# Attention, gate and experts on one core: the product with w_out as seven products of quarters, with prepared weights kept in DRAM

## The chip, the core and the metric

The kernel runs on 1 core of one Trainium2 chip. The time is that of the core on the device, in microseconds (us); 831.33 is the median of three runs, which lie between 831.1 and 831.34. TensorE (PE in the profile, its weight loads PEld) multiplies, VectorE (DVE) and ScalarE (ACT) compute on SBUF and on PSUM, where TensorE's results land, GpSimd (POOL) computes on SBUF and issues its own DMAs, and SyncE (SP) issues the other DMAs. Each engine works through its own queue in order and waits on semaphores.

## The reference, cut to what matters

Three blocks follow each other, on 1536 tokens (2 x 768) with 512 features:

```
x   = local attention of q, k, v, mem_k, mem_v           # chunks of 32 tokens, 8 heads of 64
y   = (sigmoid(x @ w_gate) * (x @ w_val)) @ w_out        # 512 -> 1536 -> 512
out = sum over 4 experts e of  p[:, e] * (relu(y @ w1[e]) @ w2[e])   # 512 -> 1024 -> 512
```

p is domain_probs divided by its row sums. Everything is float32. w_gate, w_val and w_out arrive as 64-bit floats, whose bits the kernel turns into 32-bit floats itself.

## The kernel before, in words

Every matmul operand is split into a high part (a cast to fp32r, on ACT) and a low part (the rest, a subtraction on VectorE), and a product is three matmuls: high x high, high x low, low x high (`mm3`, lines 177 to 180). TensorE's queue therefore sees triples of lines 178, 179 and 180.

The order of all work is written out by hand (`manual_schedule`): the program's order is each engine's queue order. The stages are:

- Attention, with the first value projections (`pv`) filled in between.
- The gating stage. For each of 12 row blocks f of w_out's input and three chunks c of 512 tokens, `g_part` makes the gate product, a sigmoid (line 1093) and the multiplication with the value (line 1099). The result lies in `g_t[f]`, one tile of 1536 tokens for each f. Between chunks, `dec` advances the weights of later products: per block two VectorE operations and one of ACT that rebuild 32-bit floats from the 64-bit words (lines 133, 139, 143), then the high cast and the low subtraction (lines 168, 172). A gate block f < 8 takes 12 matmuls a chunk, f >= 8 takes 24, since the value product is made there too.
- The product with w_out (`pb`, lines 1227 to 1253). For each chunk c of 512 tokens and each f, `g_split` splits the gated values three blocks ahead (lines 116 and 117) and four column blocks m of 128 are accumulated in four PSUM banks; at a chunk's end ACT copies them to `yr`. In the last chunk one step of `y_prep(0)` (the operands of the first half of y) and one of `w1_all(0)` (those of the first expert's w1) go behind each f.
- The expert block (`second_block`). Its products are already made by seven products of quarters instead of eight, with sums and differences of quarters as operands; y's seven operands for each token half are stored in DRAM (`kept_y`, line 364) and loaded back when a half is needed again.

In the last chunk VectorE's queue thus mixes three kinds of work: `hl` (gated values), `yo` and `yr` (y's operands and their sums, lines 245 and 248) and `w_s` and `raw` (w1's, lines 269 and 275). SP's queue mixes the stores of y with the loads of the raw w1 and w2 parts (lines 230 and 239). The casts of w2's first parts are made by line 332.

## Time and profile before

| what | value |
|---|---|
| time, median of 3 runs | 831.33 us |
| time of the profiled execution | 831.14 us |
| its span, first to last instruction | 829.1 us |
| TensorE busy | 823.2 us, 99% |
| VectorE busy | 541.4 us, 65% |
| ACT busy | 441.0 us, 53% |
| POOL busy | 163.8 us, 20% |
| TensorE's granted clock | 0.999 of full speed |

How to read it: an engine's busy time is a mean over stages. Whether an engine's work costs time is seen where another engine waits for it, and the row of a wait names the engine that waits, what it waits for and for how long. In the timeline the start of one matmul to the start of the next is what it costs TensorE; the recorded length overlaps with the next.

### The profile page before, as it was taken

To read this page: it belongs to the slowest core of one execution; us is meant where nothing else is said; L and a number is where in the kernel's file an instruction comes from. 1 tells how busy PE (TensorE), PEld (TensorE's weight loads), DVE (VectorE), ACT (ScalarE), POOL (GpSimd) and SP (SyncE) were. 2 spreads that over 40 slices of the span, in tenths; PEclk is the share of its full clock that TensorE was granted. 3 is DMA by queue.
4 is the path that set the end of the run, shared out by engine and by line. 5 is a ranking of instruction groups with operands and counts; after the bars stand their busy time and mean duration, and the time that the engine had idled before them with its cause. 6 is when DMAs were issued, how large, how long until landed. Compare 5 with 4: busy or idle time off the path is not lost.

```text
span 829.1 us, 14479 instructions
## 1 busy us (share of the span) xinstructions
PE 823.2 (99%) x5566; PEld 764.9 (92%) x5566; DVE 541.4 (65%) x1041; ACT 441.0 (53%) x953; POOL 163.8 (20%) x194
## 2 busy tenths in 40 slices
PE   8999999999999999999999999999999999999998
PEld 6899998888888888889899999999999999999998
DVE  7753246432343227565488788788888889888847
ACT  5764355331232326464566666666566666666642
POOL 3220000000000000010122532432342243243231
PEclk9999999999999999999999999999999999999999
DMA  9975053211110003554385794894893994994783
GB/s 345 342 284 164 2 153 117 87 51 47 56 51 1 0 1 157 211 226 168 127 308 86 121 341 62 143 346 49 164 321 42 221 268 47 261 225 54 232 193 77
DMA packets 47845, 127.47 MB, mean 154 GB/s; under 512 B 5648, under 2 KB 27552, under 8 KB 47776
## 3 DMA queue, kind: packets, MB, share of 16 engines
q1 hardware_dynamic: 23888, 102.53, 33.9%
q0 software_dynamic: 23888, 24.02, 20.5%
q8 instruction: 43, 0.70, 0.3%
q14 instruction: 26, 0.21, 0.1%
HBM read 90.35 MB, written 36.18 MB: 153 GB/s over the span
## 4 chain that ended last, share of the span: by engine, by line
PE 97%; DMA 1%; ACT 1%; DVE 1%; issue 0%; POOL 0%; SPq 0%; ACTq 0%; DVEq 0%; POOLq 0%
PE b L178 5%; PE b L179 5%; PE b L180 5%; PE B L180 5%; PE B L179 5%; PE B L178 5%; PE pv L178 4%; PE pv L180 4%; PE pv L179 4%; PE pg L180 4%; PE pg L178 4%; PE pb L180 4%; PE pb L178 4%; PE pb L179 4%; PE pg L179 4%; PE e L178 3%
## 5 line engine op out<-in xcount | busy, mean ns | idle before, releaser
L662 POOL DMA_DIRECT2D out_dram<-st x159 | 137.4, 929 | 267.6 <-DVE st L685 238.4
L178 PE MATMUL b<-yo,w_s 128*128 128x384 f32 x256 | 86.7, 339 | 0.2
L179 PE MATMUL b<-yo,w_s 128*128 128x384 f32 x256 | 86.6, 338 | 0.0
L180 PE MATMUL b<-yo,w_s 128*128 128x384 f32 x256 | 86.4, 337 | 0.0
L269 DVE TENSOR_TENSOR w_s<-raw,w_s 128x512 fp32r<-128x512 f32 x105 | 69.4, 685 | 8.9 <-ACT w_s L263 8.9
L553 POOL DMA_DIRECT2D out_dram<-st x12 | 6.5, 543 | 337.2 <-ACT st L552 337.0
L263 ACT CAST w_s<-raw 128x512 fp32r<-128x512 f32 x105 | 61.1, 618 | 14.8 <-DVE raw L275 14.7
L1093 ACT ACTIVATE sg<-pg 128x512 f32<-128x512 f32 x36 | 21.5, 598 | 84.3 <-PE pg L180 84.3
L178 PE MATMUL pv<-xs,w_v 128*128 128x384 f32 (+1 forms) x176 | 64.2, 365 | 0.0
L622 DVE SCALAR_TENSOR_TENSOR v<-v 128x384 f32<-128x384 f32 x112 | 61.9, 553 | 2.1 <-ACT v L775 0.6
L180 PE MATMUL pv<-xs,w_v 128*128 128x384 f32 (+1 forms) x176 | 61.8, 351 | 0.0
L179 PE MATMUL pv<-xs,w_v 128*128 128x384 f32 (+1 forms) x176 | 61.5, 349 | 0.0
L117 DVE TENSOR_TENSOR hl<-g,hl 128x512 fp32r<-128x512 f32 x36 | 24.7, 690 | 48.5 <-ACT hl L116 48.5
L180 PE MATMUL pg<-xs,w_g 128*128 128x512 f32 x144 | 56.0, 389 | 0.0
L179 PE MATMUL pg<-xs,w_g 128*128 128x512 f32 x144 | 56.0, 389 | 0.0
L178 PE MATMUL pb<-hl,w_o 128*128 128x512 f32 x144 | 56.0, 389 | 0.0
L179 PE MATMUL pb<-hl,w_o 128*128 128x512 f32 x144 | 56.0, 389 | 0.0
L180 PE MATMUL pb<-hl,w_o 128*128 128x512 f32 x144 | 56.0, 389 | 0.0
L178 PE MATMUL pg<-xs,w_g 128*128 128x512 f32 x144 | 56.0, 389 | 0.0
L116 ACT CAST hl<-g 128x512 fp32r<-128x512 f32 x36 | 22.2, 623 | 54.8 <-PE pb L180 54.8
L178 PEld LDWEIGHTS b<-yo,w_s 128*128 128x128 f32 x256 | 48.2, 188 | 1.3 <-ACT s L466 0.9
L179 PEld LDWEIGHTS b<-yo,w_s 128*128 128x128 f32 x256 | 48.2, 188 | 0.3
(278 smaller groups left out, 2435.5 us busy)
## 6 DMA issues: line engine op xcount, KB each, us to landing
yo<-kept_y SPq DMA_DIRECT2D x49, 768.0 KB, 10.3
out_dram<-st POOLq DMA_DIRECT2D x159, 128.0 KB, 4.6
raw<-in_w_dram SPq DMA_DIRECT2D x32, 512.0 KB, 6.9
kept_y<-yo SPq DMA_DIRECT2D x14, 768.0 KB, 4.2
kv<-in_kvc_dram SPq DMA_DIRECT2D x20, 483.0 KB, 6.0
raw<-in_w_v_dram SPq DMA_DIRECT2D x12, 512.0 KB, 6.9
raw<-in_w_g_dram SPq DMA_DIRECT2D x12, 512.0 KB, 5.5
raw<-in_w_o_dram SPq DMA_DIRECT2D x12, 512.0 KB, 3.2
```

Source lines behind the costliest of these rows:

```text
L116: nc.scalar.copy(out=hi, in_=src)
L117: nc.vector.tensor_tensor(out=lo, in0=src, in1=f32(hi), op=ALU.subtract)
L178: nc.tensor.matmul(out=ps, lhsT=w_hi, rhs=r_hi, start=first, stop=False, skip_group_check=more)
L179: nc.tensor.matmul(out=ps, lhsT=w_hi, rhs=r_lo, start=False, stop=False, skip_group_check=more)
L180: nc.tensor.matmul(out=ps, lhsT=w_lo, rhs=r_hi, start=False, stop=last, skip_group_check=more)
L263: nc.scalar.copy(out=high(t), in_=parts(n)[a])
L269: nc.vector.tensor_tensor(out=low(t), in0=parts(n)[a], in1=f32(high(t)), op=ALU.subtract)
L553: nc.gpsimd.dma_start(out=out_of(n, tt, slice(0, DM)), in_=st)
L622: nc.vector.scalar_tensor_tensor(out=out, in0=x, scalar=0.0, in1=y, op0=ALU.max, op1=op)
L662: nc.gpsimd.dma_start(out=out_of(n, t, cols_of(dh)), in_=st, accum_op=ALU.add)
L1093: nc.scalar.activation(out=sg, in_=ps, func=AF.Sigmoid)
```

## The change

The product with w_out is made in two rounds of 768 tokens. Each round makes seven products of quarters (tokens in halves of 384, w_out's rows in halves of six blocks, its columns in halves of 256), in the order 1, 7, 6, 2, 5, 4, 3 (`M_USE`). A product takes three slots c; a slot pairs row blocks and has 12 matmuls of 384 columns. The list of pieces:

- w_out is decoded in pairs (p, p + 6) of row blocks; `o_prep` makes four sums and seven operands of a pair, in eleven steps, and stores each operand to DRAM (`kept_o`, 42 stores of 256 KB). `jobs` lists these 66 steps among the nine that are left for w_gate and w_val, and a number per gating chunk is issued: one in two of three chunks for f < 4, three for f < 8, five for f < 11. `o_load` brings a product's operands back, three loads of 512 KB, issued two products ahead.
- The gated values lie in `g_t[j, f // 2]`, a tile for each token half j, so one chunk's multiplication may be cut in two. The sums of their quarters are made in place: `sum1` and `sum3` on VectorE, `sum2` and `sum4` on POOL. `o_split` splits the operand of a slot one product ahead.
- The last gating block makes its chunks 1 and 2 together, so that the tiles of x come free one by one.
- The steps of `y_prep(0)` and `w1_all(0)` go into the second round, at positions 3k + c. The sums in `y_prep(0)` are on POOL now.
- Tiles get other homes: the temporaries of attention and decoding lie in three tiles (`late`) that later hold three operands of y; weight tiles come from eight and four buffers (`w`, `ws`) in place of twelve.

The core of the diff:

```diff
+N_GV = 20
+M_USE = (1, 7, 6, 2, 5, 4, 3)
...
+    n_pr = KF // 2
+    pairs = [[("o", p), ("o", p + n_pr)] for p in range(n_pr)]
+    raw_order = order[:N_GV] + sum(pairs[:n_pr // 2], []) + order[N_GV:] + sum(pairs[n_pr // 2:], [])
+    raw_at = {key: i for i, key in enumerate(raw_order)}
...
-    def w_tile(pool, key):
-        W[key] = pool.tile([128, 2, 512], F32R, tag="w", name="w_" + "_".join(map(str, key)))
+    def w_tile(key):
+        tag, n = ("ws", 4) if NV <= order.index(key) < NV + 4 else ("w", 8)
+        W[key] = wp.tile([128, 2, 512], F32R, tag=tag, bufs=n, name="w_" + "_".join(map(str, key)))
...
+    late = ctx.enter_context(tc.tile_pool(name="late", bufs=3, side="right"))
...
+            tag, n = ("ws", 4) if 4 < made["w"] <= 8 else ("w", 8)
+            return wp.tile([128, 1024], F32R, tag=tag, bufs=n, name=f"w_s{made['w']}")
...
-        pool = tc.alloc_tile_pool(name="yo", bufs=1, side="right", reuse_waits="tile")
-        pools["yo"] = pool
         for m in (4, 5, 3):
-            op[m] = pool.tile([128, 2, 2, HT], F32R, name=f"yo{m}")
+            op[m] = late.tile([128, 2, 2, HT], F32R, tag="late", name=f"yo{m}")
...
-            q, t, do = y_sums(j, yr[j], nc.vector)
+            q, t, do = y_sums(j, yr[j], nc.gpsimd)
...
+        def g_ends(f, c, ps, val):
             sg = sgp.tile([128, CT], F32, tag="sg", bufs=3, name=f"sg{f}_{c}")
             nc.scalar.activation(out=sg, in_=ps, func=AF.Sigmoid)
-            val = g_t[f][:, ct(c)]
...
+        def g_part(f, cs):
+            todo = [("g", c, ps_tile(f"pg{f}_{c}")) for c in cs]
             if f >= NV:
...
+                todo += [("v", c, ps_tile(f"pv{f}_{c}")) for c in cs]
+            for k in range(KD):
+                for what, c, ps in todo:
+                    proj(ps, (what, f), ct(c), k)
...
+        kept_o = {m: kept.tile([128, n_pr, 2 * DH], F32, name=f"kept_o{m}") for m in M_USE}
+        DM2 = DM // 2
+        def o_prep(p):
+            t, w, o = {}, {}, []
+            def decoded(i):
+                def do():
+                    up, down = raw_parts(pairs[p][i])
+                    t2 = low_bits(down)
+                    t[i] = high_bits(i, up)
+                    joined(t[i], t2)
+                    raw_to(raw_at[pairs[p][i]] + 1 + RAWS)
+                return do
...
+            def hi(m, a):
+                def do():
+                    if len(w) % 2 == 0:
+                        o.append(wp.tile([128, 2, 2, DM2], F32R, tag="ws", bufs=4, name=f"o{p}_{m}"))
+                    w[m] = o[-1][:, len(w) % 2]
+                    nc.scalar.copy(out=w[m][:, 0], in_=part(a))
+                return do
+            def lo(m, a):
+                def do():
+                    nc.vector.tensor_tensor(out=w[m][:, 1], in0=part(a), in1=f32(w[m][:, 0]), op=ALU.subtract)
+                    nc.sync.dma_start(
+                        out=kept_o[m][:, p], in_=f32(w[m].rearrange("p l d -> p (l d)")))
+                return do
...
+            return [
+                decoded(0), decoded(1), both(hi(4, "a22"), hi(1, "a11")), both(lo(4, "a22"), s1),
+                both(hi(2, "a12"), lo(1, "a11"), s3, s2), both(lo(2, "a12"), s4), hi(7, "a21"),
+                both(hi(6, "a11"), lo(7, "a21")), both(hi(5, "a22"), lo(6, "a11")), both(hi(3, "a12"), lo(5, "a22")),
+                lo(3, "a12")]
...
+        jobs = [lambda n=n: split_f64(n) for n in range(begun[0], N_GV)] + [lambda: split_f64(N_GV, False)]
+        for p in range(n_pr // 2):
+            jobs += o_prep(p)
+        jobs += [lambda n=n: split_f64(n) for n in range(N_GV, n_64)] + [lambda: split_f64(n_64, False)]
+        for p in range(n_pr // 2, n_pr):
+            jobs += o_prep(p)
+        op_t, loaded = [], {}
+        def q_of(j, c):
+            k0, k1 = g_t[j, c], g_t[j, c + 3]
+            return dict(q00=k0[:, :, :HT], q01=k0[:, :, HT:], q10=k1[:, :, :HT], q11=k1[:, :, HT:], e=e_t[c])
+        def o_sum(j, c, eng, dst, a, b):
+            q = q_of(j, c)
+            eng.tensor_tensor(out=q[dst], in0=q[a], in1=q[b], op=ALU.subtract)
+        def sum1(j, c):
+            o_sum(j, c, nc.vector, "e", "q01", "q00")
+        def sum3(j, c):
+            o_sum(j, c, nc.vector, "q01", "q11", "q01")
+        def sum2(j, c):
+            o_sum(j, c, nc.gpsimd, "q00", "q11", "e")
+        def sum4(j, c):
+            o_sum(j, c, nc.gpsimd, "q00", "q10", "q00")
+        at_of = {1: "q00", 7: "q01", 6: "q00", 2: "q10", 5: "e", 4: "q00", 3: "q11"}
+        h_of = {}
+        def o_split(j, k, c):
+            m = M_USE[k]
+            op = op_t[(j * 7 + k) % 2 * 3 + c]
+            h_of[j, m, c] = op
+            a = q_of(j, c)[at_of[m]]
+            nc.scalar.copy(out=op[:, 0], in_=a)
+            nc.vector.tensor_tensor(out=op[:, 1], in0=a, in1=f32(op[:, 0]), op=ALU.subtract)
+        def o_load(i):
+            if i < 2 * 7:
+                m = M_USE[i % 7]
+                loaded[i] = [slot("w") for _ in range(3)]
+                for c in range(3):
+                    nc.sync.dma_start(
+                        out=f32(loaded[i][c]),
+                        in_=kept_o[m][:, 2 * c:2 * c + 2].rearrange("p a b -> p (a b)"))
+        for f in range(KF):
+            for cs in ((0,), (1,), (2,)) if f < KF - 1 else ((0,), (1, 2)):
+                ends = list(g_part(f, cs))
+                if f == KF - 1 and len(cs) > 1:
+                    ops = [xp.tile([128, 2, 2, 2, HT], F32R, tag="x", name=f"op{i}") for i in range(3)]
+                    op_t.extend(ops[i // 2][:, i % 2] for i in range(6))
+                    for c in range(3):
+                        o_split(0, 0, c)
+                for c, ps, val in ends:
+                    g_ends(f, c, ps, val)
+                n = 0
+                if f < 4:
+                    n = cs[0] != 1
+                elif f < NV:
+                    n = 3
+                elif f < KF - 1:
+                    n = 5
+                emit(jobs, n)
+                if f == NV:
+                    sum1(0, cs[0])
+                if f == NV + 1:
+                    if cs[0] == 0:
+                        sum3(0, 0)
+                if f == KF - 2 and cs[0] == 0:
+                    sum3(0, 1)
                 if f == KF - 1:
...
-            for c in range(NCT):
-                pss = [ps_tile(f"pb{c}_{m}") for m in range(KD)]
-                if c == NCT - 1:
-                    y_steps, w_steps = y_prep(0), w1_all(0)
-                for f in range(KF):
-                    i = c * KF + f
-                    g_split(i + 3)
-                    dec(begun[0])
-                    w, hl = W["o", f], hls.pop(i)
-                    for m in range(KD):
-                        mc = slice(m * 128, (m + 1) * 128)
-                        mm3(pss[m], w[:, 0, mc], w[:, 1, mc], hl[:, 0], hl[:, 1], f == 0, f == KF - 1)
-                    if c == NCT - 1:
-                        emit(y_steps, 1)
-                        emit(w_steps, 1 if f >= 2 else 0)
...
+                    if cs[0] == 0:
+                        emit(jobs, len(jobs))
+                        o_load(0)
+                        o_load(1)
+                    else:
+                        sum3(0, 2)
...
+        pos = {}
+        for j in range(NR):
+            if j == 1:
+                yr.append(xp.tile([128, KD, 2 * HT], F32, tag="x", name="yr1"))
+                yops.extend(y_ops())
+                raw1_load(0)
+                for i, do in enumerate(y_prep(0)):
+                    pos.setdefault(2 * i, []).append(do)
+                for i, steps in {
+                        8: "h4 h1", 9: "l4 s1", 10: "h2 l1 s3 s2", 11: "l2 s4", 15: "h7", 16: "h6 l7", 17: "l6 h5",
+                        18: "l5 h3", 19: "l3 x"}.items():
+                    pos.setdefault(i, []).append(lambda steps=steps: w1_do(0, steps))
+            ps = {}
+            for k, m in enumerate(M_USE):
+                i = j * 7 + k
+                o_load(i + 2)
+                name = {1: "b", 7: "e", 6: "b", 2: "a", 5: "b", 4: "e", 3: "b"}[m]
+                first = m in (1, 7, 2)
+                if first:
+                    ps[name] = [ps_tile(f"o{name}{j}_{u}") for u in range(2)]
+                if j == 0 and k == 6:
...
+                for c in range(3):
+                    if i + 1 < 2 * 7:
+                        o_split(*divmod(i + 1, 7), c)
+                    if k == 0:
+                        sum2(j, c)
+                    elif k == 1:
+                        sum4(j, c)
+                    elif j == 0 and k == 4:
+                        sum1(1, c)
+                    elif j == 0 and k == 5:
+                        sum3(1, c)
+                    if j == 1:
+                        for do in pos.get(3 * k + c, []):
+                            do()
+                    w = loaded[i][c].rearrange("p (a l d) -> p a l d", a=2, l=2)
+                    h = h_of[j, m, c]
+                    for a in range(2):
+                        for u in range(2):
+                            mc = slice(u * 128, (u + 1) * 128)
+                            n = 2 * c + a
+                            mm3(ps[name][u][:, :HT], w[:, a, 0, mc], w[:, a, 1, mc], h[:, 0, a], h[:, 1, a],
+                                first and n == 0, n == n_pr - 1, not first)
+                slots["w"].extend(loaded.pop(i))
+                for u in range(2):
+                    p = ps[name][u][:, :HT]
+                    t0, t1 = slice(0, HT), slice(HT, 2 * HT)
+                    y11, y21, y22, y12 = yr[j][:, u, t0], yr[j][:, 2 + u, t0], yr[j][:, 2 + u, t1], yr[j][:, u, t1]
+                    to = {1: y11, 7: y22, 6: y21, 2: y11, 5: y22, 4: y21, 3: y12}[m]
+                    if m in (1, 7, 6, 3):
+                        nc.scalar.copy(out=to, in_=p)
+                    else:
+                        nc.vector.tensor_tensor(out=to, in0=p, in1=to, op=ALU.add)
...
```

The scheduled orders show where this puts instructions. The first place is VectorE's queue beside the last quarter of the old product (row blocks 8 to 11 of the last chunk; `hl` is the split gated value, `yo` an operand of y, `w_s` an operand of w1, `raw1` its sums):

```order
L275 TENSOR_TENSOR raw1_0_2834<-raw1_1_2836,raw1_0_2834 128x512
L117 TENSOR_TENSOR hl32_3152<-g8_2213,hl32_3152 128x512
L245 TENSOR_TENSOR yo1_2841<-yr0_2839,yo1_2841 128x768
L269 TENSOR_TENSOR w_s3_3147<-raw1_0_2834,w_s3_3147 128x512
L275 TENSOR_TENSOR raw1_0_2834<-raw1_0_2834 128x512
L117 TENSOR_TENSOR hl33_3172<-g9_2311,hl33_3172 128x512
L245 TENSOR_TENSOR yo6_2842<-yr0_2839,yo6_2842 128x768
```

and now beside product 10, the fourth of the second round (`opb` is the split operand of product 11, one slot in a tile; the last row begins the results of product 10):

```order
L1325 TENSOR_TENSOR opb0_3030<-e0_1490,opb0_3030 128x768
L289 TENSOR_TENSOR w_s1_2633<-raw1_1_3088,w_s1_2633 128x512
L295 TENSOR_TENSOR raw1_1_3088<-raw1_1_3088 128x512
L1325 TENSOR_TENSOR opb1_3031<-e1_1491,opb1_3031 128x768
L265 TENSOR_TENSOR yo1_3081<-yr0_2715,yo1_3081 128x768
L289 TENSOR_TENSOR w_s2_2634<-raw1_0_3086,w_s2_2634 128x512
L295 TENSOR_TENSOR raw1_1_3088<-raw1_0_3086,raw1_1_3088 128x512
L295 TENSOR_TENSOR raw1_0_3086<-raw1_1_3088,raw1_0_3086 128x512
L1325 TENSOR_TENSOR opb2_3032<-e2_1492,opb2_3032 128x768
L289 TENSOR_TENSOR w_s6_2641<-raw1_0_3086,w_s6_2641 128x512
L295 TENSOR_TENSOR raw1_0_3086<-raw1_0_3086 128x512
L1429 TENSOR_TENSOR yr1_3080<-oa1_0_3263,yr1_3080 128x384
```

The splits have grown from 512 to 768 columns, y's sums (line 248 before) have left VectorE, and results of the product (line 1429) have come to it from ACT.

The second place is POOL's queue between its last low part of w_gate in the attention part and its first DMA of the expert block, before:

```order
L158 TENSOR_TENSOR w_g_2_1044<-t1_10_1004,w_g_2_1044 128x512
L158 TENSOR_TENSOR w_g_3_1141<-t1_11_1101,w_g_3_1141 128x512
L553 DMA out_0_dram<-st0_3295 128x512 x2
L553 DMA out_0_dram<-st1_3296 128x512 x2
L553 DMA out_0_dram<-st0_3295 128x512 x2
```

and now the part of the second round (`g1` is the second token half, `e` its first sum, `yr0` the first half of y):

```order
L1301 TENSOR_TENSOR g1_0_137<-g1_3_140,e0_1490 128x2x384
L1301 TENSOR_TENSOR g1_1_138<-g1_4_1656,e1_1491 128x2x384
L1301 TENSOR_TENSOR g1_2_139<-g1_5_1657,e2_1492 128x2x384
L268 TENSOR_TENSOR yr0_2715<-yr0_2715 128x2x384 x2
L1301 TENSOR_TENSOR g1_0_137<-g1_3_140,g1_0_137 128x2x384
L1301 TENSOR_TENSOR g1_1_138<-g1_4_1656,g1_1_138 128x2x384
L268 TENSOR_TENSOR yr0_2715<-yr0_2715 128x2x384
L1301 TENSOR_TENSOR g1_2_139<-g1_5_1657,g1_2_139 128x2x384
L268 TENSOR_TENSOR yr0_2715<-yr0_2715 128x2x384
```

POOL had nothing between the attention part and the expert block; it now has ten sums of 768 columns in this round, and six in the first.

The third place is SP's queue, from the stores of y to the loads of the raw w2 parts. Before, nothing stands between the last stores and the loads:

```order
L364 DMA kept_y0_78<-yo1_2841 128x1536
L364 DMA kept_y0_78<-yo6_2842 128x1536
L364 DMA kept_y0_78<-yo4_2846 128x1536
L230 DMA raw1_0_2834<-in_w_1_dram 128x1024
L230 DMA raw1_1_2836<-in_w_1_dram 128x1024
L239 DMA raw2_0_3291<-in_w_2_dram 128x1024
```

Now the operands of products 12 and 13 (`w_s` from `kept_o`) stand between the stores:

```order
L382 DMA kept_y0_83<-yo5_3084 128x1536
L1332 DMA w_s3_2635<-kept_o4_1652 128x1024
L1332 DMA w_s4_2639<-kept_o4_1652 128x1024
L1332 DMA w_s5_2640<-kept_o4_1652 128x1024
L382 DMA kept_y0_83<-yo1_3081 128x1536
L1332 DMA w_s7_2716<-kept_o3_1653 128x1024
L1332 DMA w_s8_2717<-kept_o3_1653 128x1024
L1332 DMA w_s9_2718<-kept_o3_1653 128x1024
L382 DMA kept_y0_83<-yo6_3082 128x1536
L382 DMA kept_y0_83<-yo4_3083 128x1536
L250 DMA raw1_0_3086<-in_w_1_dram 128x1024
L250 DMA raw1_1_3088<-in_w_1_dram 128x1024
```

Each product's loads are now queued behind a store that waits for a low part of y.

## Rows read from the trace of the kernel before

**Rows 1.** The page, engines' shares (busy us, share, instructions) and the chain by engine

```profile
PE 823.2 (99%) x5566; PEld 764.9 (92%) x5566; DVE 541.4 (65%) x1041; ACT 441.0 (53%) x953; POOL 163.8 (20%) x194
...
PE 97%; DMA 1%; ACT 1%; DVE 1%; issue 0%; POOL 0%; SPq 0%; ACTq 0%; DVEq 0%; POOLq 0%
```

**Rows 2.** Waits of TensorE: total us, times, longest

```profile
PE warm L964 <- DVE zero L1110: 1.1, 1, 1.1
```

**Rows 3.** Timeline of TensorE: start us, us, instruction; the old product's ends

```profile
247.11 0.39 PE L178 MATMUL pb<-hl,w_o 128*128 128x512 f32 x1
...
345.03 0.33 PE L178 MATMUL b<-yo,w_s 128*128 128x384 f32 x1
...
346.10 0.33 PE L178 MATMUL e<-yo,w_s 128*128 128x384 f32 x1
...
348.18 0.33 PE L178 MATMUL b<-yo,w_s 128*128 128x384 f32 x1
...
351.34 0.34 PE L178 MATMUL b<-yo,w_s 128*128 128x384 f32 x1
```

**Rows 4.** The tile pb: count, ns min/median/max, first and last start

```profile
L180 PE MATMUL pb<-hl,w_o x144: 389/389/389, 247.6 to 344.8; 128*128 128x512 f32 x144
```

**Rows 5.** Busy us of each engine in stretches; granted clock, DMA share, GB/s

```profile
130.00:150.00 20.00, 20.00 (x90) 16.57 (x89) 11.49 (x20) 9.11 (x16) 0.00 (x0) 1.00 0.41 131
...
313.00:345.03 32.03, 32.03 (x144) 26.50 (x142) 22.93 (x32) 16.18 (x27) 0.00 (x0) 1.00 0.60 236
...
550.00:600.00 50.00, 50.00 (x348) 49.90 (x347) 41.85 (x79) 31.14 (x68) 18.15 (x21) 1.00 0.70 139
```

**Rows 6.** Timeline of VectorE: operations of 768, 512 and 384 columns

```profile
329.68 0.95 DVE L245 TENSOR_TENSOR yo<-yr,yo 128x768 fp32r<-128x768 f32 x1
330.55 0.68 DVE L269 TENSOR_TENSOR w_s<-raw,w_s 128x512 fp32r<-128x512 f32 x1
...
335.42 0.68 DVE L117 TENSOR_TENSOR hl<-g,hl 128x512 fp32r<-128x512 f32 x1
336.02 0.68 DVE L269 TENSOR_TENSOR w_s<-raw,w_s 128x512 fp32r<-128x512 f32 x1
...
351.05 0.55 DVE L492 TENSOR_TENSOR v<-a,s 128x384 f32<-128x384 f32 x1
351.52 0.55 DVE L492 TENSOR_TENSOR v<-e,s 128x384 f32<-128x384 f32 x1
```

**Rows 7.** Timeline of ACT: a cast of 768 columns, copies of 384

```profile
321.27 0.83 ACT L242 CAST yo<-yr 128x768 fp32r<-128x768 f32 x1
...
346.29 0.48 ACT L466 COPY s<-b 128x384 f32<-128x384 f32 x1 [0.48 <-PE b L180]
...
354.19 0.47 ACT L466 COPY s<-b 128x384 f32<-128x384 f32 x1
354.56 0.48 ACT L466 COPY s<-e 128x384 f32<-128x384 f32 x1
```

**Rows 8.** Timeline of POOL and VectorE in the attention part

```profile
13.29 1.28 POOL L158 TENSOR_TENSOR w_v<-t,w_v 128x512 fp32r<-128x512 f32 x1 [8.21 <-ACT w_v L157]
...
13.78 0.81 DVE L1003 TENSOR_SCALAR nm<-nm 128x6 f32<-128x6 f32 x1
...
39.70 0.17 DVE L1003 TENSOR_SCALAR nm<-nm 128x6 f32<-128x6 f32 x1
```

**Rows 9.** The chain that ended last, 349 to 355 us: start us, us, what

```profile
349.79 0.63 ACT w_s L332
...
354.72 0.44 PE b L178
```

**Rows 10.** Timeline of SP's queue, 300 to 372 us: loads of w1, then w2

```profile
337.94 0.81 SPq L230 DMA_DIRECT2D raw<-in_w_dram  x2
338.84 23.10 SPq L239 DMA_DIRECT2D raw<-in_w_dram  x4
```

**Rows 11.** The line of the raw w2 loads: from issue to landing

```profile
DMA to landing us min/median/max: 3.3/7.4/9.5
```

More of the change, by code (lines that the diff above doesn't have):

```diff
@@ L100, in fused_kernel @@
         order += [("g", f), ("v", f)]
-    order += [("o", f) for f in range(KF)]
     n_64 = len(order)
+    n_pr = KF // 2
+    pairs = [[("o", p), ("o", p + n_pr)] for p in range(n_pr)]
+    raw_order = order[:N_GV] + sum(pairs[:n_pr // 2], []) + order[N_GV:] + sum(pairs[n_pr // 2:], [])
+    raw_at = {key: i for i, key in enumerate(raw_order)}
     src = {"g": w_g, "v": w_v, "o": w_o}
@@ L106, in raw_to @@
     def raw_to(n):
-        while len(raws) < min(n, n_64):
+        while len(raws) < min(n, len(raw_order)):
             i = len(raws)
             r = rawp.tile([128, 1024], U32, tag="raw", name=f"raw{i}")
-            nc.sync.dma_start(out=r, in_=src[order[i][0]][order[i][1]].bitcast(U32))
+            what, f = raw_order[i]
+            nc.sync.dma_start(out=r, in_=src[what][f].bitcast(U32))
             raws.append(r)
@@ new lines, in fused_kernel @@
+        gpool[0, "b"] = tc.alloc_tile_pool(name="g0b", bufs=(KF - NV) // 2)
+        gpool[1, "b"] = tc.alloc_tile_pool(name="g1b", bufs=(KF - NV) // 2, side="right")
+        e_pool = tc.alloc_tile_pool(name="ep", bufs=3, side="right")
+        sgp = tc.alloc_tile_pool(name="sgp", bufs=3, side="right")
+        e_t = [e_pool.tile([128, 2, HT], F32, tag="e", name=f"e{c}") for c in range(3)]
+        banks[1] = ctx.enter_context(tc.tile_pool(name="ps_n", bufs=5, space=PSUM))
+        for f in range(NV):
+            for _ in v_part(NBLK - 1, [(f, k) for k in range(KD)]):
+                pass
+            dec(min(12 + f + 1, 2 * NV))
```

168 lines of the change are left out of this document (81 added, 87 removed).

## The prediction

> **What bounds the kernel now.** I read the page's shares first, then the chain of waits, then TensorE's own waits, then its instructions in order of time around the product with w_out. TensorE is busy for 823.2 of 829.1 us and holds 97% of the chain that ended last [rows 1]; the longest of its three recorded waits is 1.1 us, at the start [rows 2]. So a microsecond of matmul taken away is a microsecond gained, if nothing else takes the place. The product with w_out starts at 247.11 us and gives way to the first matmul of the expert block at 345.03 [rows 3]: 97.92 us, in three groups of 144 matmuls of 512 columns of which one is shown [rows 4], 226.7 ns apart (97.92 / 432). VectorE has slack there: in the last third, where it also prepares the next block, it is busy 22.93 of 32.03 us [rows 5].
>
> **TensorE's part.** Two token rounds x 7 products x 3 slots x 2 quarter rows x 2 column halves x 3 matmuls make 504 matmuls of 384 columns in place of 432 of 512. The same form stands right behind the old product: 36 of them from 345.03 to 351.34, 175.3 ns apart [rows 3]. The first six take 178 ns each (345.03 to 346.10), the next twelve 173.3 (to 348.18) [rows 3]. 504 x 175.3 = 88.35 us, so 9.6 us go; by the two ends 8.1 or 10.6. One product is 36 x 175.3 ns = 6.31 us. Regrouping the last gating matmuls so that x is free earlier changes neither their number nor their shape: 0.
>
> **Preparing w_out.** A pair of row blocks now takes 4 operations of 512 and 11 of 256 columns on VectorE. VectorE starts operations of 768, 512 and 384 columns 0.87, 0.60 and 0.47 us apart [rows 6]; 256 columns I estimate from these at 0.33. A pair is then 6.0 us. In gating blocks 4 to 7 nine of a pair's eleven steps are issued in one block of 36 matmuls (8.2 us): 4.9 us, and 1.9 for gating itself, of 8.2. The stretch of before with most of this work had 11.49 of 20.00 us on VectorE and 41% DMA [rows 5]. It fits, barely. The 75 steps run out in the first chunk of block 10; five chunks of 24 matmuls, 27 us, lie between that and the first product, and hide what runs late. Were this cover gone, every microsecond beyond the 27 would be one of TensorE. Cost 0. The 42 stores and 42 loads stand on SP's queue; their pace is a rival below. The attention part keeps its order and its waits, only tiles get other homes: 0; a cost would show as a new wait of TensorE there.
>
> **Operands and results inside the products.** Each product needs three high casts (0.83 us, ACT), three low subtractions (0.87 us apart, VectorE) and two results of 384 columns, on ACT or VectorE (0.37 and 0.47 apart) [rows 6, 7]. That is at most 3.6 us of VectorE in 6.31, one product ahead: hidden. In the first round two products also carry three sums each (2.6 us more, 6.2 of 6.31), but the lead of one product covers them: 0. Their operands alternate between two sets of three, so a cast also waits for the product before last, which is past.
>
> **The second round, where it gets narrow.** Here VectorE also prepares y and w1, and POOL does ten sums of 768 columns. I count from the start of product 0. Product 7 starts at 7 x 6.31 = 44.2. ACT takes 0.2 us to see the end of product 6 (346.10 to 346.29) [rows 3, 7], then 2 x 0.37 for the results and 0.83 for a cast, so VectorE starts the low parts of product 8 at about 46.0. Before product 12 can start it must do 18 operations of 768 columns (products 8 to 11 three each and the first of 12 make 13; five low parts of y), seven of 512 for w1 and two results: 18 x 0.87 + 7 x 0.60 + 2 x 0.47 = 20.8 us. Product 12 is due at 12 x 6.31 = 75.7, so there are 29.7 us, 8.9 to spare. In the same stretch POOL does seven sums (four of y, three of the operands). A POOL subtraction of 512 columns took 1.28 us [rows 8]; 768 columns make 1.92 as an estimate in proportion, 13.4 for seven.
>
> The question is whether the two engines work side by side. No row shows a VectorE subtraction of two SBUF operands beside a POOL one. The nearest rows show a small VectorE operation that takes 0.17 us at 39.70, but 0.81 where it started at 13.78 inside a POOL subtraction (13.29 to 14.57), until 14.59 [rows 8]: it waited for POOL. The two ends are 0 (side by side) and 13.4 - 8.9 = 4.5, plus 1.9 if an eighth sum still runs when the stretch begins: 6.4. I take the nearest row at its word, less the last 0.1 us of each POOL record, in which the small operation already ran: 12.7 - 8.9 = 3.8 us lost.
>
> The Trainium skill (SBUF — State Buffer, Who interferes with whom) says that a VectorE instruction with two SBUF inputs contends with a GpSimd instruction that reads SBUF, the later one blocked for the whole instruction; no run here shows it for this form, and by it the loss is the 4.5 above and without it 0. The Trainium skill (GPSIMD Engine Reference, Engine selection) would keep such sums on VectorE, where it finds them about twice as fast; the trace agrees with 0.68 to 1.28 us, and seven sums of 0.87 on VectorE would fit the 8.9 us, so this rule speaks against the change's move of y's sums to POOL.
>
> **Sum.** 831.14 us of the profiled execution (829.1 of span and 2.0 around it) - 9.6 + 3.8 = 825.3; that execution lies 0.19 under the median of the runs, which makes 825.5.
>
> **Rivals.**
> Side by side: POOL does not hold VectorE up. Then nothing fills the 29.7 us and only the matmuls count: 831.33 - 9.6 = 821.7. For it: the one blocked operation has another form than the subtractions. Against it: it is the only overlap inside a POOL record that there is to read.
>
> The hand-over to the expert block. Before, ACT's cast of the raw w2 parts at 349.79, 4.76 us behind the last product, opens a chain over VectorE and ACT that ends in TensorE waiting at 354.72 [rows 9], so any delay there is paid in full. Its loads follow those of w1, issued at 337.94, 7.1 us ahead of the hand-over [rows 10]. Now the w1 loads wait for the last w1 low part, behind product 12's two results: 0.2 + 0.94 + 2 x 0.60 = 2.4 us into product 13, so 3.9 ahead of the hand-over. With the second pair issued 0.8 us later, and 7.4 us to landing in the median and 9.5 at most [rows 11], they land 4.3 or 6.4 behind it: in time by 0.5, or 1.6 late; with VectorE late by another 2 us, 3.6 late. Together with the 6.4 of POOL this is 831.33 - 9.6 + 6.4 + 3.6 = 831.7, no change.
>
> Weights too slow (slower): each product wants three loads of 0.52 MB, 1.57 MB in 6.31 us, 249 GB/s; in the second round seven stores of y (0.79 MB each) and two loads of w1 share SP's one queue, and the weights of product 12 are issued only behind the store that waits for y's fifth low part. With 3.8 us lost to POOL, 5.8 us are left to lose, 0.41 per product: the kernel gets slower if a product's weights need over 6.7 us, under 234 GB/s. The DMAs' pace at full share was 131 / 0.41 = 320 GB/s with 4 KB rows, 236 / 0.60 = 393 in the last third, and 139 / 0.70 = 199 in the expert block, where small accumulating stores run too [rows 5]. At 199 a product takes 7.9 us, and 14 x 1.6 = 22 us put the time at 848. For it: the new stores have 2 KB rows, which none of these stretches shows. Against it: loads are issued two to three products ahead, and the pure load stretches are above 249.
>
> **How the numbers follow.** Forecast (POOL holds VectorE, 823 to 828): 0.52. Side by side: 0.28. Hand-over on top (828 to 833): 0.10. Weights: 0.10. The likeliest is 825.5. Its own range with the matmul ends (8.1 to 10.6) and the POOL ends is 820.7 to 829.6; the range 820.9 to 829.9 holds the first two cases and a little of the third, some 8 in 10. About 0.2% (1.7 us) is what can be told from no change: faster is both first cases and a quarter of the third, 0.83; same 0.07; slower 0.10.
>
> **What would show it.** Right: 504 matmuls some 175 ns apart; VectorE's low subtractions and POOL's sums never overlapping, or those that overlap with two to three times their 0.95 us; TensorE waits, some 4 us in all, in products 9 to 12 of the second round on VectorE's low parts, and none in the first round. Side by side is right if subtractions keep 0.95 us next to POOL. The hand-over would show as a wait of the w2 cast on its DMA. Weights would show as TensorE waiting for a DMA at the first matmul of a slot. I am wrong altogether if TensorE waits in gating blocks 4 to 10, for weights not yet prepared or a PSUM bank not yet freed, or if 384-column matmuls stand over 194 ns apart, where 504 of them cost what 432 did.

## The result, and the profile after

| | before | after |
|---|---|---|
| time, median (us) | 831.22 | 823.98 (823.52 to 824.54) |
| ratio, 95% interval | | 0.9914 [0.9897, 0.9931] |
| profiled execution: time / span | 831.14 / 829.1 | 824.09 / 822.3 |
| ahead of the product with w_out | 247.11 | 247.53 |
| product, first matmul to first one of the expert block | 97.92 | 91.57 |
| from there to the end of the span | 484.07 | 483.20 |

7.2 us were gained; 825.5 had been forecast, in a range from 820.9 to 829.9. The gain lies in the product: 6.35 of the 6.8 us of the span.

The page of the changed kernel (shares of the engines, then the chain) answers to [rows 1]:

```profile
PE 813.1 (99%) x5638; PEld 769.7 (94%) x5638; DVE 603.2 (73%) x1133; ACT 460.3 (56%) x989; POOL 201.2 (24%) x210
...
PE 94%; DVE 2%; DMA 2%; ACT 1%; issue 1%; SPq 0%; ACTq 0%; DVEq 0%
```

TensorE's own waits over the whole span (us in total, times, longest) answer to [rows 2]:

```profile
PE oa L197 <- DVE opb L1325: 1.2, 2, 1.0
PE warm L981 <- DVE tmp L1137: 1.1, 1, 1.1
PE ob L197 <- DVE opb L1325: 1.1, 1, 1.1
PE oe L197 <- DVE opb L1325: 0.8, 1, 0.8
...
```

TensorE still holds the chain, but the shares of VectorE and of the DMAs in it each went from 1% to 2%, and three groups of waits on the low parts of the operands (L1325) are new. No wait names a DMA of weights, and none lies in the gating blocks or the first round. TensorE's instructions in order of time (start, duration, what; in brackets the wait before it) answer to [rows 3]:

```profile
247.53 0.33 PE L196 MATMUL ob<-op,w_s 128*128 128x384 f32 x1
...
291.24 0.33 PE L196 MATMUL ob<-opb,w_s 128*128 128x384 f32 x1
...
313.43 0.44 PE L197 MATMUL oa<-opb,w_s 128*128 128x384 f32 x1 [1.04 <-DVE opb L1325]
...
315.95 0.44 PE L197 MATMUL oa<-opb,w_s 128*128 128x384 f32 x1 [0.16 <-DVE opb L1325]
...
323.55 0.44 PE L197 MATMUL ob<-opb,w_s 128*128 128x384 f32 x1 [1.08 <-DVE opb L1325]
...
326.68 0.44 PE L197 MATMUL oe<-opb,w_s 128*128 128x384 f32 x1 [0.77 <-DVE opb L1325]
...
339.10 0.33 PE L196 MATMUL b<-yo,w_s 128*128 128x384 f32 x1
```

The first round takes 43.71 us (247.53 to 291.24), 252 matmuls 173.4 ns apart. The second takes 47.86: the same 43.71 and 4.15 us of waits. The four rows with a bracket are in products 10, 11 and 12 (counted from 0). With each, the next start comes later than 173.4 ns by 1.21, 0.33, 1.25 and 0.94 us, 3.73 in all; the rest of the 4.15 is 0.1 us or so behind each wait.

VectorE (first fence) and POOL (second) in the same stretch of the second round answer to [rows 6, 8]; `x2` stands for two instructions in a row:

```profile
298.92 3.48 DVE L1325 TENSOR_TENSOR opb<-g,opb 128x768 fp32r<-128x768 f32 x2 [1.96 <-ACT opb L1324]
302.33 2.60 DVE L265 TENSOR_TENSOR yo<-yr,yo 128x768 fp32r<-128x768 f32 x1
304.85 5.13 DVE L1325 TENSOR_TENSOR opb<-g,opb 128x768 fp32r<-128x768 f32 x2
309.91 2.60 DVE L265 TENSOR_TENSOR yo<-yr,yo 128x768 fp32r<-128x768 f32 x1
```

```profile
301.56 5.09 POOL L1301 TENSOR_TENSOR g<-g,g 128x768 f32<-128x768 f32 x2
306.60 2.57 POOL L268 TENSOR_TENSOR yr<-yr 128x768 f32<-128x768 f32 x1
309.12 2.57 POOL L1301 TENSOR_TENSOR g<-g,g 128x768 f32<-128x768 f32 x1
```

A VectorE subtraction that takes 0.95 us alone takes 2.60 beside a POOL sum, and a POOL sum 2.57. Each holds the other up: VectorE does one subtraction per POOL sum, though a sum that meets none takes 1.85 us, the least of y's four sums (min, median and max in ns):

```profile
L268 POOL TENSOR_TENSOR yr<-yr x4: 1854/2478/2571, 297.1 to 312.7; 128x768 f32<-128x768 f32 x4
```

The groups by line over the product (count, busy time, mean ns, idle time before) show how much that is:

```profile
L1325 DVE TENSOR_TENSOR opb<-g,opb 128x768 fp32r<-128x768 f32 x18 | 25.4, 1449 | 4.6 <-ACT opb L1324 4.6
L265 DVE TENSOR_TENSOR yo<-yr,yo 128x768 fp32r<-128x768 f32 x7 | 9.9, 1420 | 0.0
```

The windows by stage answer to [rows 5]; the columns are stretch, length, busy time of PE, PEld, DVE, ACT and POOL, granted clock, DMA share and GB/s:

```profile
247.53:291.24 43.71, 43.71 (x253) 43.70 (x252) 34.40 (x37) 18.78 (x28) 13.21 (x6) 1.00 0.82 264
291.24:339.10 47.86, 44.80 (x253) 43.46 (x253) 42.21 (x42) 26.46 (x41) 19.21 (x9) 1.00 0.70 253
```

The hand-over to the expert block answers to [rows 9]; from the chain of waits of the changed kernel:

```profile
343.46 0.48 ACT s L484
343.94 0.53 ACT w_s L352
...
348.76 0.44 PE b L196
```

The cast of the raw w2 parts (L352) comes 4.84 us behind the last product, as before (4.76), right behind a copy of ACT, without a wait for its load. The second of these casts does wait for its load, for 0.21 us:

```profile
344.66 0.62 ACT L352 CAST w_s<-raw 128x512 fp32r<-128x512 f32 x1 [0.21 <-DMA raw<-in_w_dram]
```

This costs nothing: ACT's next instruction waits another 0.40 us for VectorE, and TensorE waits for nothing there. The raw loads of w1 (L250) and w2 (L259) and the loads of weights answer to [rows 10, 11], from SyncE's queue and from the page:

```profile
337.00 0.81 SPq L250 DMA_DIRECT2D raw<-in_w_dram  x2
337.91 0.84 SPq L259 DMA_DIRECT2D raw<-in_w_dram  x2
```

```profile
w_s<-kept_o SPq DMA_DIRECT2D x42, 512.0 KB, 5.8
```

### The profile page after: what moved, and what is told of

It is laid out like the page before. It is cut to its first block, busy times and chain, and to the rows that moved or that the text cites. A ratio compares the mean times of both kernels' runs of the same rounds, so it can differ in the third digit from the quotient of the medians.

```text
span 822.3 us, 15033 instructions
## 1 busy us (share of the span) xinstructions
PE 813.1 (99%) x5638; PEld 769.7 (94%) x5638; DVE 603.2 (73%) x1133; ACT 460.3 (56%) x989; POOL 201.2 (24%) x210
## 3 DMA queue, kind: packets, MB, share of 16 engines
q0 software_dynamic: 23888, 24.02, 20.8%
## 4 chain that ended last, share of the span: by engine, by line
PE 94%; DVE 2%; DMA 2%; ACT 1%; issue 1%; SPq 0%; ACTq 0%; DVEq 0%
PE b L196 5%; PE b L197 5%; PE b L198 5%; PE B L198 5%; PE B L197 5%; PE B L196 5%; PE pv L196 4%; PE pv L198 4%; PE pv L197 4%; PE pg L196 4%; PE pg L197 4%; PE pg L198 4%; PE e L196 3%; PE e L197 3%; PE e L198 3%; PE E L198 2%
## 5 line engine op out<-in xcount | busy, mean ns | idle before, releaser
L680 POOL DMA_DIRECT2D out_dram<-st x159 | 137.4, 928 | 266.6 <-DVE st L703 237.6
L1301 POOL TENSOR_TENSOR g<-g,e 128x768 f32<-128x768 f32 x6 | 13.7, 2292 | 197.7 <-DVE op L1325 173.0
L196 PEld LDWEIGHTS b<-yo,w_s 128*128 128x128 f32 x256 | 48.1, 188 | 1.5 <-ACT s L484 1.1
L197 PEld LDWEIGHTS b<-yo,w_s 128*128 128x128 f32 x256 | 48.2, 188 | 0.3
L198 PE MATMUL B<-w_s,h 128*128 128x256 f32 x171 | 48.3, 282 | 0.0
L197 PE MATMUL B<-w_s,h 128*128 128x256 f32 x171 | 48.2, 282 | 0.0
L196 PE MATMUL B<-w_s,h 128*128 128x256 f32 x171 | 48.1, 281 | 0.0
L198 PEld LDWEIGHTS b<-yo,w_s 128*128 128x128 f32 x256 | 48.1, 188 | 0.0
L198 PE MATMUL B<-w_s,hx 128*128 128x256 f32 x165 | 46.6, 282 | 0.0
## 6 DMA issues: line engine op xcount, KB each, us to landing
kv<-in_kvc_dram SPq DMA_DIRECT2D x20, 483.0 KB, 6.3
```

Of the source, the lines that this page charges most:

```text
L196: nc.tensor.matmul(out=ps, lhsT=w_hi, rhs=r_hi, start=first, stop=False, skip_group_check=more)
L197: nc.tensor.matmul(out=ps, lhsT=w_hi, rhs=r_lo, start=False, stop=False, skip_group_check=more)
L198: nc.tensor.matmul(out=ps, lhsT=w_lo, rhs=r_hi, start=False, stop=last, skip_group_check=more)
L680: nc.gpsimd.dma_start(out=out_of(n, t, cols_of(dh)), in_=st, accum_op=ALU.add)
L1301: eng.tensor_tensor(out=q[dst], in0=q[a], in1=q[b], op=ALU.subtract)
```

## Experiments

All times are medians of the runs of a kernel; "product" is the stretch of the table above, read from the profile of each.

| kernel | time (us) | product (us) | TensorE held up in it by |
|---|---|---|---|
| before / after | 831.2 / 824.0 | 97.92 / 91.57 | - / VectorE |
| y sums on VectorE | 820.6 | 88.48 | VectorE, once |
| operand sums on VectorE | 823.2 | 91.01 | VectorE |
| all sums on VectorE | 820.1 | 88.46 | VectorE, once |
| the same with spare POOL sums | 836.6 | 104.66 | VectorE |
| the same with spare POOL copies | 826.3 | 94.07 | VectorE |
| the same, w1 steps later | 821.0 | 87.48 | nothing |
| the same, six weight slots | 825.4 | 93.11 | DMA, ACT once |
| before, y sums on POOL | 831.5 | 97.92 | nothing |
| early w1 / and w2 loaded first | 823.2 / 822.8 | 90.86 / 90.87 | VectorE |

**Who does the sums.** The theory of the prediction is that POOL's sums and VectorE's subtractions shut each other out. The rival: they work side by side, and the order of the queues or VectorE's load is what TensorE waits for. Three kernels move one kind of sum or both.

```diff
-            q, t, do = y_sums(j, yr[j], nc.gpsimd)
+            q, t, do = y_sums(j, yr[j], nc.vector)
```

> The four sums of y (768 columns each) go from POOL back to VectorE; the six operand sums of each round stay on POOL. The changed kernel has 824.0 us, of which 3.7 us are TensorE waits on VectorE's low parts in the second round. Theory (a POOL sum and a VectorE subtraction of two SBUF operands shut each other out): VectorE's work before the product in which the waits end grows by 4 x 0.87 = 3.5 us, but four POOL sums of 1.85 us no longer stand in its way, 7.4 us; the balance of 3.9 us takes nearly all of the waits away: 820 to 821.5 us, TensorE waits in the second round under 1.2 us. Rival (order and load: the two engines work side by side, VectorE and ACT hand operands to each other too late, and POOL's help is what keeps VectorE from being later still): VectorE gets 3.5 us more, so the waits grow: 825 to 827.5 us.

```diff
-            o_sum(j, c, nc.gpsimd, "q00", "q11", "e")
+            o_sum(j, c, nc.vector, "q00", "q11", "e")
-            o_sum(j, c, nc.gpsimd, "q00", "q10", "q00")
+            o_sum(j, c, nc.vector, "q00", "q10", "q00")
```

> The six operand sums of each round go to VectorE, the four sums of y stay on POOL. Theory (shutting out): in the stretch of the second round VectorE's work grows by three sums, 2.6 us, and three POOL sums, 5.5 us, no longer stand in its way: of 3.7 us of waits about 0.8 are left: 820.5 to 822 us; the low subtractions that still take over 2 us stand beside a sum of y only. Rival (order and load): 825 to 827 us.

Both edits:

> All sums (four of y, six operand sums in each round) on VectorE; POOL does none inside the product with w_out. Theory (POOL and VectorE shut each other out): no VectorE subtraction of 768 columns takes more than 1.0 us (now up to 2.6), VectorE's work before the last waits grows by 7 x 0.87 = 6.1 us, to 26.9 us of 29.7, so nothing is left to wait for: 819.5 to 821 us, TensorE waits in the second round under 0.6 us. Rival (order and load): 8.7 us more of VectorE work in the second round, waits of 6 to 12 us: 826 to 833 us. A third reading (POOL's 2.5 us sums deliver their results late, and whoever needs these waits): as the theory, 820 to 821.5; the run with spare sums tells it apart.

Measured: 820.6 us (0.9866 of before [0.9852, 0.988]), 823.2 (0.9896 [0.9883, 0.9909]) and 820.1 (0.9859 [0.9846, 0.9871]). VectorE got more to do each time, and the kernel became faster each time. With all sums on VectorE its groups in the product are at their own pace:

```profile
L1325 DVE TENSOR_TENSOR opb<-g,opb 128x768 fp32r<-128x768 f32 x18 | 16.7, 950 | 4.3 <-ACT opb L1324 4.3
L265 DVE TENSOR_TENSOR yo<-yr,yo 128x768 fp32r<-128x768 f32 x7 | 6.7, 951 | 0.0
```

TensorE's waits from 247 to 345 us in that kernel:

```profile
PE oe L197 <- DVE opb L1325: 0.8, 1, 0.8
```

One wait is left. The two groups take 11.9 us less than in the changed kernel, for 8.7 us of VectorE work added in the second round (ten sums). So POOL's help took more from VectorE than it gave. One size was wrong: with y's sums alone left on POOL I had expected waits of 0.8 us, and the product shows 2.55 over the kernel without POOL sums (91.01 against 88.46), while the operand sums alone cost nothing (88.48). The count of VectorE's work over the whole stretch misses where its idle time lies. In the kernel with operand sums alone on POOL three of the six run in products 6 and 7, ahead of the stretch, and the other three hold up three operations there (2.60, 2.49 and 2.60 us); y's four sums stand in products 8 to 10. That the place makes the difference is argued from this, not shown: no run moves the sums in time alone.

**The instruction or its result.** A late result of POOL could also be what the others wait for. So with all sums on VectorE, POOL does ten subtractions that nobody reads:

```diff
+        def spare(c, low):
+            out = yr[1][:, 0:2, HT:2 * HT]
+            nc.gpsimd.tensor_tensor(out=out, in0=q_of(1, c)["q10"], in1=low, op=ALU.subtract)
...
+                    if j == 1 and k < 2:
+                        spare(c, f32(op_t[(7 + k + 1) % 2 * 3 + c][:, 1]))
...
+                        for ym in {2: (1, 1), 4: (3,), 6: (2,)}.get(n, ()):
+                            spare(c, f32(yops[0][ym][:, 1]))
```

> All sums on VectorE, and in the second round POOL does ten spare subtractions of 768 columns at the places where it did sums (each reads the low part that VectorE has just written, and writes a quarter of the second round's result that is written only later): nobody waits for their results. Theory (POOL instructions themselves shut VectorE out): about seven of the ten fall into the stretch, 13 us, on top of 26.9 us of VectorE work in 29.7 us: 10 us lost against the kernel with all sums on VectorE, 828 to 832 us, and VectorE's low subtractions take up to 2.6 us again. Rival (late results): nobody needs these results, so the same time as the kernel with all sums on VectorE, within 0.7 us of it, and no VectorE subtraction over 1.0 us.

836.6 us (1.0067 [1.0049, 1.0086]): 16.5 us slower than without them. The rival of late results is out: the trace has no instruction that waits for a spare sum. (The profiled execution of this kernel also had a granted clock of 0.95 in its first 100 us, so only its product is read here.) It is more than the 10 us expected, which had seven of the ten sums in the stretch; all ten ran ahead of the wait that ended at 332.70, the last until 331.83, and 1.65 us each make 16.5. Of the 16.2 us by which the product is longer, 1.6 per spare sum, TensorE's waits are 11.9 more (12.7 against 0.8); most of the rest is the clock. TensorE at the end of the longest wait:

```profile
314.37 0.69 PE L197 MATMUL ob<-opb,w_s 128*128 128x384 f32 x1 [5.80 <-DVE opb L1329]
314.86 0.53 PE L198 MATMUL ob<-opb,w_s 128*128 128x384 f32 x1
```

Windows of that wait, of the stretch behind it, and of the stretch behind another wait of 1.9 us that ended at 332.70:

```profile
308.40:314.30 5.90, 0.17 (x1) 0.00 (x0) 5.87 (x3) 5.28 (x8) 4.93 (x2) 0.74 0.87 302
314.30:317.70 3.40, 3.33 (x10) 3.33 (x11) 3.37 (x3) 0.00 (x0) 2.53 (x1) 0.50 0.42 172
332.70:336.10 3.40, 3.40 (x19) 3.40 (x20) 3.37 (x5) 2.16 (x3) 0.00 (x0) 1.00 0.28 112
```

After 5.80 us of standing idle the granted clock is 0.50 (1.2 GHz), and matmuls start 0.32 us apart in place of 0.173; behind the wait of 1.9 us it is 1.00.

**The form of the POOL instruction.** The same kernel with copies of one operand:

```diff
-            nc.gpsimd.tensor_tensor(out=out, in0=q_of(1, c)["q10"], in1=low, op=ALU.subtract)
+            nc.gpsimd.tensor_scalar(out=out, in0=low, scalar1=1.0, scalar2=None, op0=ALU.mult)
```

> All sums on VectorE, and at the ten places where the run with spare sums did POOL subtractions of two operands, POOL now does spare copies of one operand (times 1.0, 768 columns, no one waits for them). Theory A (any POOL work that reads SBUF shuts VectorE's subtractions out): as with the spare sums, 832 to 838 us, VectorE's low subtractions up to 2.6 us. Theory B (only POOL instructions with two SBUF operands do): as with all sums on VectorE, 820.1 us within 0.7, no VectorE subtraction over 1.0 us.

826.3 us (0.9937 [0.9925, 0.9949]), between the two theories: the product is 5.6 us longer than without them, some 0.6 us per copy. VectorE (first fence) and POOL (second):

```profile
306.97 1.47 DVE L1301 TENSOR_TENSOR g<-g,g 128x768 f32<-128x768 f32 x1
308.36 0.95 DVE L265 TENSOR_TENSOR yo<-yr,yo 128x768 fp32r<-128x768 f32 x1
```

```profile
306.65 4.65 POOL L1317 TENSOR_SCALAR yr<-opb 128x768 f32<-128x768 f32 x2
```

During a copy of 2.3 us two subtractions run, of which one takes 0.5 to 0.6 us longer; during a sum only one does. A copy holds VectorE up too, but for a part of its time.

**The same move in the kernel before.** Its diff is that of y's sums, with the engines exchanged.

> The kernel before, with one part of the change alone: the four sums of y on POOL in place of VectorE. Theory (shutting out, and it costs only what VectorE has not to spare): four POOL sums of 1.85 us cost VectorE 7.4 us less 3.5 us that it no longer does, 3.9 us of the 9.1 us it had idle in the last third of the old product: 831.3 us, no change, while single VectorE subtractions beside a POOL sum take up to 2.6 us. Rival (a POOL sum of y costs its own time wherever it stands): 4 us slower, 835.

831.5 us (1.0002 [0.9991, 1.0012]), product 97.92 as before. VectorE's low parts of y by line, with min, median and max ns:

```profile
L245 DVE TENSOR_TENSOR yo<-yr,yo x14: 947/950/2606, 316.6 to 367.3; 128x768 fp32r<-128x768 f32 x14
```

They shut each other out there too (2606 ns), and it cost nothing: VectorE had the time to spare.

**The wait that is left.** With all sums on VectorE, TensorE still loses 0.94 us in product 12.

```diff
-                        8: "h4 h1", 9: "l4 s1", 10: "h2 l1 s3 s2", 11: "l2 s4", 15: "h7", ...
+                        8: "h4 h1", 9: "l4 s1", 12: "h2 l1 s3 s2", 13: "l2 s4", 15: "h7", ...
```

> All sums on VectorE, and the five w1 steps that stood in front of the first low part of the last product but one come behind it. The wait of 0.8 us that is left there with all sums on VectorE: if it is VectorE's queue that is full (five operations of 512 columns, 0.60 us apart, stand ahead: 3.0 us), the wait goes and nothing new takes its place: 819.0 to 819.6 us against 820.1. If instead ACT's cast or the product's two results decide when that low part can start, the wait stays: 820.1.

821.0 us (0.987 [0.9857, 0.9882]), no gain, though the product shrinks to 87.48 us without a wait. So that wait was VectorE's queue, as expected: one cast of ACT moved along with the five steps, but with all sums on VectorE that queue, by its rows, waits for nothing from 292.01 to the low part in question, at 321.88. "Nothing new takes its place" was wrong. TensorE's waits around the hand-over, which came at 335.44, and the chain there:

```profile
PE b L196 <- DVE v L510: 0.5, 1, 0.5
```

```profile
335.17 0.38 SPq L259
...
335.61 6.51 DMA raw<-in_w_dram
...
342.20 0.62 ACT w_s L352
```

The w2 load goes out no later, 87.2 us after the product's first matmul as with all sums on VectorE (335.17 - 247.96 and 334.10 - 246.86), since it follows VectorE's last w1 step, and VectorE has the same work and no wait up to it in either kernel. But the hand-over comes 0.98 us earlier, and the cast now waits for its load: the rival "hand-over", present as soon as the product is fast enough. From the hand-over to the end takes 483.76 us here, 483.08 with all sums on VectorE, so 0.3 of the 0.98 us should be left. That no gain shows lies in the start of the product in the two executions, 247.96 and 246.86; a second execution of the kernel with all sums on VectorE has it at 247.55. Two more kernels tried to have both, beside the base and the changed kernel on one chip.

> The changed kernel itself, unaltered, beside the three variants of this group on one chip: 824.0 us within 0.6, some 7 to 8 us under the kernel before.

> All sums on VectorE once more, as the base of the two variants beside it: 820.1 us within 0.6, that is 3.9 us under the changed kernel on this chip. The rival (order and load) would have it at or above the changed kernel.

```diff
-                    if k == 0:
-                        sum2(j, c)
+                    if j == 0 and k == 0:
+                        sum2(0, c)
+                    elif j == 0 and k == 6:
+                        sum2(1, c)
...
-                        8: "h4 h1", 9: "l4 s1", 10: "h2 l1 s3 s2", 11: "l2 s4", 15: "h7", ...
+                        0: "h4 h1", 1: "l4 s1", 2: "h2 l1", 3: "s3 s2", 5: "l2 s4", 15: "h7", ...
```

> All sums on VectorE; the second round's first three operand sums (2.6 us) move into the last product of the first round, and the first half of the w1 steps (seven operations of 512 columns, 4.2 us) moves from the third and fourth product of the second round to the first and second, where VectorE had 7.3 us idle. If VectorE's backlog before the last product but one is what TensorE's last wait of 0.8 us rests on, that wait goes without making the expert block's loads later (moving the steps back instead put 0.5 us of new waits at the hand-over): 0.9 us under the kernel with all sums on VectorE, 819.2 us. If the wait rests on the order of casts on ACT, it stays: no difference. If the early w1 steps take weight slots that the loads need, TensorE waits for a DMA: slower.

```diff
-                        18: "l5 h3", 19: "l3 x"}.items():
+                        18: "l5 h3", 19: "l3"}.items():
...
         raw2_load(0)
+        w1_do(0, "x")
```

> As the variant with early w1 steps, but at the hand-over to the expert block the raw w2 pair (1 MB) is loaded ahead of the next raw w1 pair and no longer behind it. Before, the w2 load was issued 0.9 us after the w1 load and landed 6.5 us later. If the landing of w2 at the hand-over costs TensorE anything, this takes up to 0.4 us off: 818.8 us against 819.2; if the chain over ACT's copies and VectorE is late by itself, no difference. If the w1 pair is now late for its own steps, TensorE waits in the first groups of the expert block: slower by up to 2 us.

824.4 for the changed kernel, 820.4 (0.9867 [0.9847, 0.9888]) with all sums on VectorE, 823.2 (0.9898 [0.988, 0.9917]) and 822.8 (0.9894 [0.9875, 0.9912]). The early w1 steps were a miss. Their expectation had 7.3 us of idle time in products 7 and 8; with all sums on VectorE the trace has 1.6 there (10.90 of 12.48 us busy), and the three sums that moved out made room for 2.6 more. The wait in product 12 went, but products 9 and 10 got new ones. TensorE's waits, and VectorE at the start of the second round:

```profile
PE ob L197 <- DVE opb L1325: 1.4, 1, 1.4
PE oa L197 <- DVE opb L1325: 1.2, 2, 0.8
```

```profile
292.61 0.96 DVE L1325 TENSOR_TENSOR opb<-g,opb 128x768 fp32r<-128x768 f32 x1 [1.34 <-ACT opb L1324]
295.12 0.96 DVE L1325 TENSOR_TENSOR opb<-g,opb 128x768 fp32r<-128x768 f32 x1 [1.55 <-ACT opb L1324]
295.99 0.69 DVE L289 TENSOR_TENSOR w_s<-raw,w_s 128x512 fp32r<-128x512 f32 x1
```

VectorE still stands idle for ACT's casts, which now also come behind early w1 casts; its queue is in order, so the w1 steps that follow a low part do not fill that idle time: 3.0 us are idle in products 7 and 8 (9.46 of 12.48 us busy). The order of the w2 and w1 loads made no difference that can be told (their times overlap). So the best kernel found is the change with all sums on VectorE: 820.4 us against 824.4 and, before, 831.0 on one chip.

**Weights.** 

```diff
-                loaded[i] = [slot("w") for _ in range(3)]
+                loaded[i] = [slot("w") if i < 2 else slots["w"].pop(0) for _ in range(3)]
...
-                o_load(i + 2)
+                if i:
+                    o_load(i + 1)
```

> All sums on VectorE; the weights of the product with w_out go through six slots in place of twelve, so a product's three loads are issued when the product before it starts, and cannot land earlier. Theory (DMA has the pace, the rival of slow weights was wrong at its root): a load lands 5.8 us after issue in the median, under the 6.24 us of a product: 820 to 823 us. Rival (it is the lead of the twelve slots that hides a DMA slower than TensorE: 1.57 MB per product plus 0.79 MB of y stores): the weights come 1 to 3 us late in most of the twelve products that follow: 828 to 850 us, and TensorE waits for a DMA of w_s from kept_o.

825.4 us (0.992 [0.9908, 0.9932]), 5.3 over the base, between the two. TensorE's waits in the product:

```profile
PE ob L196 <- DMA w_s<-kept_o: 2.8, 2, 1.8
PE ob L196 <- ACT yr L1428: 0.6, 1, 0.6
PE oe L196 <- DMA w_s<-kept_o: 0.4, 1, 0.4
PE oa L196 <- DMA w_s<-kept_o: 0.4, 2, 0.2
```

All of these waits lie in the second round, where y's stores share the queue: there the weights do come late by up to 1.8 us once the lead of twelve slots is gone. In the first round even six slots are enough. The DMA is not all of it. A load takes longer to land in the second round (median 7.0 us, against 4.4 in the first), but it also goes out late, behind a store in SyncE's queue that waits for a low part of y. The chain ahead of the longest wait, which ended at 319.83:

```profile
313.67 0.28 SPq L382
...
314.04 5.66 DMA w_s<-kept_o
```

Product 10 had begun at 311.10; the load for product 11 left 2.9 us later, when VectorE had ended a low part of y at 313.56, and then landed in 5.66 us, less than the 6.24 of a product. Ahead of product 13 (a wait of 1.0 us) the load left 0.6 us after product 12 began and took 6.74 us to land. No run separates the two causes.

## Why the prediction came out right, step by step

- **TensorE's part** (-9.6, ends 8.1 and 10.6): 504 x 173.4 ns is 87.4 us, so -10.5. The 36 matmuls that it averaged held slow ones of 178 ns; the new product runs like the fast ones of [rows 3] throughout.
- **Preparing w_out, operand splits, first round** (0): the first round has no wait at all, although the low parts there were also held up (L1325 took up to 2598 ns). The lead of a product covers it, as the prediction said.
- **The second round** (+3.8): 4.15 us, at the place and by the wait that were named, and shutting out was taken rightly from the one blocked operation in [rows 8]. But only 3.1 of it (91.57 - 88.46) goes when POOL does no sums. The rest, 1.05, is VectorE's own queue at the start of product 12 (0.94, and 0.11 behind it), which the count gave as covered; the kernels with some sums, none or spare ones on POOL all show 0.91 to 0.94 us there. That count, 20.8 us of work in 29.7, was the weak step: it treats idle time in the stretch as usable wherever it lies. Part of the agreement is luck, for two errors offset each other: in the stretch six subtractions were held up (9.9 us lost, not 12.7), and not all of the 8.9 us to spare could be used, since 1.96 of them passed in a wait for ACT's cast (298.92). By the same count that leaves 9.9 - 6.9 = 3.0.
- **Tiles that only get other homes** (0): from the hand-over on the span is 0.87 us shorter. Matmul by matmul, the 1152 there that write b and e from y's operands start 0.95 ns closer together on average (1.1 us). Every kernel with the new product shows 483.0 to 483.3 us there, save the one whose loads are late (483.76); the kernel before with y's sums on POOL shows 484.08. That it is the tiles' places was not tried and is open; the 0 of the prediction had no row that tested it.
- **Sum**: -10.5 + 4.15 + 0.4 (start) - 0.9 = -6.8 of the span, where -5.8 had been forecast. The start shows no effect of the change that can be told: it lies between 246.6 and 248.0 in the profiles with the new product, save that of the spare sums, whose clock began low.
- **Rivals**: side by side is wrong (2.60 us, and 1.6 us lost per spare sum, the lower clock included). The hand-over cost nothing, but it was near: the loads went out only 2.1 us ahead of it (337.00) and not 3.9, as VectorE ended its w1 steps 1.7 us later than counted, and one cast of w2 waited 0.21 us for its load, the sign that the prediction had named. By the prediction's median of 7.4 us the load would have been over 1 us late; it landed within 6.3. The rival costs time once the product is 4 us shorter. Weights did not show either: a load of w_s from kept_o landed 5.8 us after issue in the median, and the twelve slots hide what is late. The kernel with six slots says that this rival was near, in part by the order of SyncE's queue (a load that left 2.9 us late).

The Trainium skill (SBUF — State Buffer, Who interferes with whom) lets the instruction that came first keep the shared access for its whole length; the trace agrees for POOL sums (0.95 us became 2.60), not for POOL copies, which cost some 0.6 of their 2.3 us. Its choice of VectorE for such sums (GPSIMD Engine Reference, Engine selection) is borne out by 3.9 us.

## What to carry to other kernels

Work given to POOL is not free for VectorE where both read two operands from SBUF: count a POOL sum as time taken from VectorE (1.65 us for a sum of 1.85 here, and 0.5 to 0.6 for a copy), and give it away only where VectorE stands idle at that very time. Spare time is worth only where it lies in an in-order queue; moving work towards idle time fails if that idle time is a wait of the same queue. With a wait removed, the next one (here the w2 load at the hand-over) can take its gain, so read what is late next. A queue of loads is in order too: a load leaves only when the store ahead of it may.

## What was not expected of the hardware

- Beside VectorE, POOL's copy of one operand of 768 columns took 2.3 us, hardly less than its subtraction of two (2.4 to 2.6, and 1.85 where nothing met it), and still cost the kernel much less: 0.6 against 1.6 us of product each, of which some 0.3 are the lower clock's.
- After 5.80 us without work TensorE's granted clock was 0.50 for the 3.4 us that followed: a long wait cost more than its own length.
